# Loop matmuls on 64-row by 32-column tiles with swapped row halves, and table additions by accumulating DMAs

## The chip, the cores and the metric

The kernel runs on one core of one Trainium2 chip. The metric is device time of that core, in microseconds (us). Names of the profile: PE is TensorE, PEld its weight loads, DVE VectorE, ACT ScalarE, POOL GpSimd, SP SyncE.

## What is computed

Two independent layers on a sequence of 2,048 positions and 576 channels, their outputs side by side:

```python
# A: a diagonal state-space layer, as a causal convolution (128 states)
P = exp(dt*A[:, :, None] * l)                  # 576 x 128 x 2048, complex
K = einsum("dn,dnl,dn->dl", C, P, dt*B).real   # a kernel of 2048 taps for each channel
y = causal_conv(u, K) + u * Dskip              # by FFT in the reference
# B: attention, 32 heads of 18, one shared key and value head
q, k, v = x @ wq, x @ wk, x @ wv
p = softmax(q @ k.T * 18**-0.5)
out = concat_heads(p @ v) @ wo
```

## The kernel before, in words

**Attention** is one long loop over 4 chunks of 512 queries, 8 groups of 4 heads, 16 blocks of 128 keys and the 2 pairs of heads in a group: 1,024 exponentials of 128 x 1,024 elements on ACT (L538, L536). Ahead of each stands a *score* `s` on PE (L527: 8 matmuls in fp16 on tiles of 64 rows by 32 columns, 512 columns each), into one of two PSUM slots. After two exponentials stands a *product* `ops` (L836: 8 fp32 matmuls on tiles of the same shape, 512 columns each; an fp32 matmul shows as two records, each with its weight load). The P buffers between are ten.

**Everything else on PE is filler** between scores and products, and before the change it runs on tiles of 128 rows by 32 columns, four matmuls at a time (`matmul4`, L203): the query projection `q` (`qproj`, L418: 10 units of 256 columns for each of 19 blocks, half as many in the narrow fifth ones), the output projection `op` (`outproj`, 3 chunks x 40 units of 288 columns, and `outproj_part`, 24 units for the fourth chunk), and the convolution's three kinds: `kg` (L1260, the taps of a block of channels from two tables), the transforms `lu`, `hu`, `lk`, `hk` of input and taps, and the inverse `iy`. A unit is one visit of a filler to PE, or a part of it. The contraction of 576 channels is four blocks of 128 rows and one of 64, padded with zeros to 128.

**PSUM**: two double banks for scores, one for `ops`, one bank "a" for attention's fillers and one bank "c" for the convolution's. A filler's result is read out by DVE before its bank is filled again.

**The convolution's tables** are made on DVE (`tables`): 12 blocks of 48 channels, each in 2 parts; for each part a low table of 24 x 24 elements in a partition and a high table in two pieces of 24 x 32 and 24 x 24. A complex product costs three multiplications and two additions (L128), so each of the three pieces is five passes. `kgen` multiplies low by high.

**The order** of PE, ACT and DVE is written by a planner at build time (`main`, with the model clock `Clock`). It keeps a model time for PE, DVE and ACT and takes at each step the next score, product or filler unit; the engines then run their lists in order. It adds 0.12 us to the model whenever the row count of the tiles changes (`Clock.tile`, SWITCH). Before the change it puts a filler first where ACT has work enough left, then a score whose slot is free, then a product whenever one is due. The convolution is held to a pace of DVE work for each step (RATE = 1.9). POOL and SP issue the DMAs; POOL's are the stores of projected queries to DRAM (`qd`, L468, L506).

## Time and profile before

| | |
|---|---|
| median of 3 runs | 1172.84 us (1171.32 to 1174.79) |
| profiled execution, own time | 1173.67 us |
| its span, first to last instruction | 1171.9 us |
| granted TensorE clock, mean | 0.991 |
| DMA, mean | 72 GB/s |

The profile gives the busy time of each engine, groups of instructions by line and tile, who waited for whom, and a timeline in which instructions of one kind in a row are merged (start, time from the first start to the last end, engine, line, names, xcount). Ends of matmuls are modelled, so two starts in a row say more of PE than a duration.

### The profile page before, as it was taken

The numbers are of one execution on the slowest core, as the hardware profiler recorded it, in microseconds if no ns is written. First come the engines' busy times: TensorE is split into PE (matmuls) and PEld (weight loads), VectorE is DVE, ScalarE is ACT, GpSimd is POOL, SyncE is SP. The second block draws the span as 40 slices with busy tenths as digits, with TensorE's granted clock in tenths as the row PEclk, the third lists the DMA queues.
The fourth block names the chain that finished last, engine by engine and source line by source line (L and its number), as shares of the span: only waits on it lengthen the run. The fifth ranks groups of instructions, "written<-read, shape, count | busy, mean of one in ns | idle before, by whom it ended". The sixth has DMA issues, their size and how long they took to land.

```text
span 1171.9 us, 53466 instructions
## 1 busy us (share of the span) xinstructions
PE 1107.6 (95%) x24126; PEld 419.0 (36%) x24126; DVE 1015.0 (87%) x1713; ACT 1040.0 (89%) x1052; POOL 141.6 (12%) x257
## 2 busy tenths in 40 slices
PE   6899999999999999999899999999988999999986
PEld 2333333333333333433333333333333333333323
DVE  4868998998998997998899897998789899799583
ACT  3789999998999998999899999888899999999980
POOL 5303310112210100010401100001120000000000
PEclk9999999999999999999999999999999999999998
DMA  7412512113222003131412202113222210302101
GB/s 222 132 49 80 175 29 83 47 44 103 88 69 96 28 32 97 62 112 29 131 47 89 75 25 75 57 40 82 69 68 74 66 36 22 103 30 76 59 21 65
DMA packets 59358, 84.66 MB, mean 72 GB/s; under 512 B 14867, under 2 KB 35335, under 8 KB 58613
## 3 DMA queue, kind: packets, MB, share of 16 engines
q1 hardware_dynamic: 47557, 73.24, 19.5%
q0 software_dynamic: 10848, 7.37, 2.5%
q8 instruction: 190, 3.11, 1.1%
q10 hardware_dynamic: 720, 0.58, 0.2%
q14 instruction: 43, 0.35, 0.1%
HBM read 46.59 MB, written 33.85 MB: 69 GB/s over the span
## 4 chain that ended last, share of the span: by engine, by line
PE 66%; ACT 19%; DVE 7%; issue 4%; DMA 3%; SPq 0%; ACTq 0%; DVEq 0%
PE ops L836 24%; ACT P L538 18%; PE s L527 17%; PE q L418 6%; PE op L203 5%; PE iy L203 3%; PE kg L1260 3%; PE lk L203 2%; PE hk L203 1%; PE lu L203 1%; PE hu L203 1%; DMA xr<-xT 1%; ACT P L536 1%; PE fin L203 1%; DVE t L128 1%
## 5 line engine op out<-in xcount | busy, mean ns | idle before, releaser
L538 ACT ACTIVATE P<-s 128x1024 f32<-128x1024 f32 x992 | 975.8, 1028 | 69.3 <-PE ops L836 17.8
L836 PE MATMUL ops<-P,v_sb 64*32 64x512 f32 x8192 | 539.2, 593 | 1.9 <-DVE u L1050 1.4
L527 PE MATMUL s<-aug,kaug 55*32 55x512 f16 x8192 | 417.6, 383 | 33.1 <-ACT P L538 28.0
L527 PEld LDWEIGHTS <-kaug 55*32 55x32 f16 x8192 | 134.9, 90 | 386.8 <-issue 375.9
L836 PEld LDWEIGHTS ops<-P,v_sb 64*32 64x32 f32 x8192 | 146.9, 106 | 75.8 <-issue 46.0
L468 POOL DMA_DIRECT2D qd<-qh x116 | 66.2, 578 | 412.9 <-DVE qh L136 410.0
L418 PE MATMUL q<-x,wq_sb 128*32 128x256 f32 x1360 | 104.1, 389 | 0.4 <-DVE un L144 0.4
L203 PE MATMUL op<-wo_sb,oT 126*32 126x288 f32 (+1 forms) x1056 | 88.2, 416 | 0.0
L128 DVE TENSOR_TENSOR tab<-tab,tt 128x576 f32<-128x576 f32 (+1 forms) x72 | 59.2, 822 | 2.0
L128 DVE TENSOR_TENSOR tab<-fr,dif 128x576 f32<-128x576 f32 (+1 forms) x72 | 58.7, 815 | 0.0
L128 DVE TENSOR_TENSOR tt<-fr,sum 128x576 f32<-128x576 f32 (+1 forms) x72 | 58.7, 815 | 0.0
L128 DVE TENSOR_TENSOR tab<-sum,fr 128x576 f32<-128x576 f32 (+1 forms) x72 | 58.7, 815 | 0.0
L128 DVE TENSOR_TENSOR tab<-tab 128x576 f32<-128x576 f32 (+1 forms) x72 | 58.6, 814 | 0.0
L418 PEld LDWEIGHTS q<-x,wq_sb 128*32 128x32 f32 x1360 | 29.4, 108 | 71.5 <-issue 64.2
L1171 POOL MEMSET fr<- 128x192 f32 x24 | 9.9, 495 | 371.5 <-DVE tt L128 239.4
L203 PE MATMUL iy<-w,dft_sb 128*32 128x192 f32 x768 | 41.6, 340 | 8.6 <-DVE u L128 8.6
L128 DVE TENSOR_TENSOR acc<-acc,pt 128x1728 f32<-128x1728 f32 (+2 forms) x36 | 48.7, 1354 | 0.7
L128 DVE TENSOR_TENSOR pt<-us,ks 128x1728 f32<-128x1728 f32 (+2 forms) x36 | 48.0, 1351 | 0.3
L536 ACT ACTIVATE P<-s,bias 128x1024 f32<-128x1024 f32 x32 | 32.9, 1124 | 16.6 <-PE s L527 10.6
L132 DVE COPY ksb<-kg 128x192 f32<-128x192 f32 x48 | 17.3, 360 | 33.3 <-PE kg L1260 33.0
L203 PEld LDWEIGHTS op<-wo_sb,oT 126*32 126x32 f32 (+1 forms) x1056 | 22.9, 108 | 60.7 <-issue 50.7
L1260 PEld LDWEIGHTS kg<-tab 128*32 128x32 f32 x2304 | 35.0, 110 | 25.0 <-issue 14.6
(167 smaller groups left out, 1039.5 us busy)
## 6 DMA issues: line engine op xcount, KB each, us to landing
od<-o SPq DMA_DIRECT2D x31, 256.0 KB
aug<-qd SPq DMA_DIRECT2D x124, 55.0 KB
u<-u SPq DMA_DIRECT2D x12, 384.0 KB
kd<-ksb SPq DMA_DIRECT2D x12, 384.0 KB
kt<-kd SPq DMA_DIRECT2D x48, 96.0 KB
outa<-u SPq DMA_DIRECT2D x12, 384.0 KB
pw<-pw SPq DMA_DIRECT2D x8, 528.0 KB
oT<-od SPq DMA_DIRECT2D x16, 252.0 KB
```

Source lines behind the costliest of these rows:

```text
L128: return self.v.tensor_tensor(out, *a, **k)
L132: return self.v.tensor_copy(out, *a, **k)
L203: nc.tensor.matmul(ps[j:e], w[:, j:e], x, start=start, stop=stop, tile_position=(0, j))
L418: nc.tensor.matmul(ps[o, 256 * f:256 * f + 256], w[:, k, i], xt[:, k, x], start=(k == 0), stop=(k == 4), tile_position=(0, 32 * j))
L468: q.dma_start(qd[h:h + n, row + d:row + d + nd, cs], src[i1:i1 + n * nd, :cs.stop - cs.start])
L527: nc.tensor.matmul(ps[e:e + 32, j, :], self.kaug[r, kb * P + e:kb * P + e + 32], t[r, :], start=True, stop=True, tile_position=(64 * j, e))
L536: nc.scalar.activation(pt, ps, AF.Exp, bias=self.bias, scale=SCALE / QQ)
L538: nc.scalar.activation(pt, ps, AF.Exp, scale=SCALE / QQ)
L836: nc.tensor.matmul(o_ps[32 * j:32 * j + 32, b, cs], self.v[r, kb, :], pts[2 * pi + j // 2][r, j % 2, cs], start=(kb == 0), stop=(kb == 15) ...
L1171: nc.gpsimd.memset(t[:, :, 0:NF:8], one)
L1260: nc.tensor.matmul(ps[32 * g:32 * g + 32, d, :], t[:, :32], t[:, 32:], start=(j == 0), stop=(j == 1), tile_position=(0, 32 * g))
```

## The change

**Tiles.** All fillers of the loop run on tiles of 64 rows by 32 columns (`halves`): eight matmuls at once, the upper 64 rows of the contraction for one half of the output columns into one PSUM bank, the lower 64 rows for the other half into the next bank; then, in a second pass, the row halves are swapped, so that each bank gets the rest of its sum. So a unit holds twice as many matmuls over the same number of streamed columns for each. Between the two passes of a result stands a `drain` of PE (`flush`): once for each of 19 `q`, 12 `op`, 12 `op` parts, 24 `kg`, 48 transforms (now `dtu` and `dtk`) and 12 `iy`, 127 in all. The 64 real rows of the last contraction block are now held twice, in both halves of the partitions, so that `q` and the three whole chunks of `op` have 9 units where they had 10 (weights and rows of `op` are laid out anew for that). Only the small `up` and the tail's `fin` stay on 128 rows.

**PSUM.** The banks "a" and "c" become one pair of banks, which one filler at a time holds, from its first unit until DVE has read it.

**Tables.** The two high pieces keep their three multiplications (on halves of 24 x 32 and 24 x 24), but the additions go: two DMAs issued by POOL add on arrival, each 128 x 1,344 elements of fp32, the second of them after the first, since it writes what the first reads. The sign is moved into the factors (`sum`, now in two operations). Four small copies stand where two stood. The planner takes the tables for usable 9 us (LANDS) after the last multiplication of the high pieces; the low piece is made in that time.

**Planner.** P buffers 9 for 10; RATE 2.5 for 1.9; a score whose slot is free comes first (unless DVE is about to run dry), and a product or filler starts only where it ends within 0.2 us of the moment at which the model's ACT, less 0.3 us, has nothing left. Setup loads the double rows by a few more DMAs; `wo` is loaded in the new layout and once more in the old for the last chunk.

The core of the diff:

```diff
-NP = 10
+NP = 9
...
-RATE = 1.9
+RATE = 2.5
...
-DRY = 1.0
-ENTER = 0.7
-EDGE = 0.25
-STAY = 0.4
+DRY = 0.6
+EDGE = 0.3
+URGE = 0.2
+OVER = 0.2
...
+LANDS = 9.0
...
-    def tile(self, rows):
-        if rows != self.tiling:
-            self.tiling, self.t = rows, self.t + SWITCH
...
+def halves(nc, ps, cols, w, x, swap, start, stop):
+    for j in range(0, P, 32):
+        for b in range(2):
+            r, i = slice(64 * b, 64 * b + 64), b ^ swap
+            nc.tensor.matmul(ps[j:j + 32, i, cols], w(r, i, j), x(r, i, j), start=start, stop=stop, tile_position=(64 * b, j))
...
-        self.ps_f = {b: pool(f"ps_f{b}", 1, space=PSUM) for b in "ac"}
+        self.ps_f = pool("ps_f", 1, space=PSUM)
...
+    def pair(self, n, name):
+        self.k.pe(0.0, self.k.fill)
+        t = self.ps_f.tile([P, 2, CT], F32, tag="f", name=name)
+        return t[:, :, :n]
+    def flush(self):
+        self.nc.tensor.drain()
+        self.k.pe(0.12)
...
+        for swap, k in [(0, k) for k in range(5)] + [(1, k) for k in range(4)]:
+            def wi(r, i, j):
+                return w[r, k, j:j + 32] if m < 4 else w[r, k, j % 64:j % 64 + 32]
+            def xi(r, i, j):
+                x0 = 256 * i if m < 4 else 256 * (j // 64) + 128 * i
+                return xt[r, k, x0:x0 + n]
+            if (swap, k) == (1, 0):
+                self.flush()
+            halves(nc, ps, slice(0, n), wi, xi, swap, (swap, k) == (0, 0), (swap, k) == (1, 3))
+            K.pe(0.43 * n / 256)
+            self.q_left -= n / 256
+            self.units += n / 256
...
+            ps = self.pair(288, f"op{c}_{t}")
+            for swap, k in [(0, k) for k in range(5)] + [(1, k) for k in range(4)]:
+                if (swap, k) == (1, 0):
+                    self.flush()
+                halves(nc, ps, slice(0, 288), lambda r, i, j: o[r, k, t * P + j:t * P + j + 32],
+                       lambda r, i, j: w[r, k, 288 * i:288 * i + 288], swap, (swap, k) == (0, 0), (swap, k) == (1, 3))
...
+            last = (K.a if si < n_s else 1e9) - EDGE
+            st = choose()
+            if free <= K.t and not (st is not None and st is not side and K.v < K.t + DRY and K.t + 0.45 <= last + URGE):
+                score()
+                continue
+            if wanted(st) and K.t + 0.45 <= last + (URGE if st is not side and K.v < K.t + DRY else OVER):
                 conv.count(st)
-            elif free <= K.t:
-                score()
-            elif due() <= K.t:
+            elif due() <= K.t and K.t + 0.86 / SPLIT <= last + OVER:
                 product()
+            elif st is not None and K.t + 0.45 <= last + OVER:
+                conv.count(st)
             else:
...
+        add = lambda out, x: nc.gpsimd.dma_start(flat(out), flat(x), accum_op=ALU.add)
+        halves = ((0, 4), (4, 7))
+        for j0, j1 in halves:
+            tt(hi[:, 1, 1 + j0:1 + j1], L(r, j1 - j0), H(df, 1, j0, j1), op=ALU.mult)
             yield "v", 0.0, False
-            tt(re, L(sm), H(r), op=ALU.mult)
+            tt(hi[:, 0, 1 + j0:1 + j1], L(sm, j1 - j0), H(r, 17, j0, j1), op=ALU.mult)
+            if j0:
+                add(hi[:, 1, 1:], hi[:, 0, 1:])
             yield "v", 0.0, False
-            tt(t, L(f), H(sm), op=ALU.mult)
+        for j0, j1 in halves:
+            tt(t[:, j0:j1], L(f, j1 - j0), H(sm, 17, j0, j1), op=ALU.mult)
+            if j0:
+                add(hi[:, 0, 1:], t)
             yield "v", 0.0, False
-            tt(im, im, re, op=ALU.add)
-            yield "v", 0.0, False
-            tt(re, re, t, op=ALU.subtract)
-            if (lo, j0) != (8, 4):
-                yield "v", 0.0, False
+        self.tab_ready = K.v + LANDS
+        for j, x in enumerate((r, f)):
+            V.tensor_copy(lo[:, j, :, 0:8], x[:, :, 0:8])
+            V.tensor_copy(hi[:, j, 0], x[:, :, 8:16])
...
+        ps = self.at.pair(n * 64, f"kg{k}_{s}")
+        for swap in range(2):
+            for d in range(n):
+                at = lambda i, j: j // 32 * TB + i * n + d
+                for x in range(2):
+                    if (swap, d, x) == (1, 0, 0):
+                        self.at.flush()
+                    halves(nc, ps, slice(64 * d, 64 * d + 64), lambda r, i, j: lo[r, x, at(i, j), :], lambda r, i, j: hi[r, x, :, at(i, j), :],
+                           swap, (swap, d, x) == (0, 0, 0), (swap, d, x) == (1, n - 1, 1))
+            K.pe(0.665)
+            if swap == 0:
+                yield "p", 0.0, True
...
+            ps = self.at.pair(2 * NE, f"dt{nm}{j}")
+            for swap, h in ((0, 0), (0, 1), (1, 0), (1, 1)):
+                if (swap, h) == (1, 0):
+                    self.at.flush()
+                halves(nc, ps, slice(h * NE, h * NE + NE), lambda r, i, e: self.dft[r, (4 * j + 2 * h + i) * P + e:(4 * j + 2 * h + i) * P + e + 32],
+                       lambda r, i, e: src(r, 2 * h + i), swap, (swap, h) == (0, 0), (swap, h) == (1, 1))
+                K.pe(0.33)
+                if (swap, h) != (1, 1):
+                    yield "p", 0.0, True
+            self.evacuate()
+            V.tensor_copy(x, ps[:, :, NE:])
+            V.tensor_tensor(ac[:, 2 * j:2 * j + 2, :], ps[:, :, 0:NE], x, op=ALU.add)
+            V.tensor_tensor(bd[:, 0:4:3, :] if j == 0 else bd[:, 1:3, :], ps[:, :, 0:NE], x, op=ALU.subtract)
+            self.evacuated()```

On PE, at the taps of a block (`kg`, third block, between the scores `s` of two key blocks; the second number after the names is columns). Before:

```order
L527 MATMUL s_7_5_2712<-aug_115,kaug 32x512
L1260 MATMUL kg_0_0_2723<-tab_0_2425 32x64 [waits DVE_49]
L1260 MATMUL kg_0_0_2723<-tab_0_2425 32x64 x23
...
L836 MATMUL ops_3_2588<-P_6_4_2666,v_sb 32x512 x4
L836 MATMUL ops_3_2588<-P_7_4_2682,v_sb 32x512 x4
...
L1260 MATMUL kg_0_1_2782<-tab_0_2425 32x64 [waits DVE_49]
L1260 MATMUL kg_0_1_2782<-tab_0_2425 32x64 x23
```

And after the change, at the same block:

```order
L550 MATMUL s_7_5_3084<-aug_112,kaug 32x512
L205 MATMUL kg_0_3097<-tab_0_2737 32x64 [waits DMASW0_49,DVE_49]
L205 MATMUL kg_0_3097<-tab_0_2737 32x64 x7
L205 MATMUL kg_0_3097<-tab_0_2737 32x64 [waits DMASW7_49]
L205 MATMUL kg_0_3097<-tab_0_2737 32x64 x39
...
L205 MATMUL kg_0_3097<-tab_0_2737 32x64 x48
```

Two results of 24 matmuls have become one of 96, in two halves of 48; its first matmul waits for the two adding DMAs (DMASW) where it waited for DVE alone, and the second half stands one score later with no product between.

On DVE, the passes of one table (`tab`; `tt` and `th` are the third products). Before, the two high pieces:

```order
L128 TENSOR_TENSOR tab_0_4122<-fr_3761,dif_4007 128x24x32
L128 TENSOR_TENSOR tab_0_4122<-sum_4006,fr_3761 128x24x32
L128 TENSOR_TENSOR tt_0_8_0_4253<-fr_3761,sum_4006 128x768 [waits DVE_49]
L128 TENSOR_TENSOR tab_0_4122<-tab_0_4122 128x24x32 [waits DVE_49]
L128 TENSOR_TENSOR tab_0_4122<-tab_0_4122,tt_0_8_0_4253 128x24x32 [waits DVE_49]
L128 TENSOR_TENSOR tab_0_4122<-fr_3761,dif_4007 128x24x24
L128 TENSOR_TENSOR tab_0_4122<-sum_4006,fr_3761 128x24x24
L128 TENSOR_TENSOR tt_0_8_4_4335<-fr_3761,sum_4006 128x576 [waits DVE_49]
L128 TENSOR_TENSOR tab_0_4122<-tab_0_4122 128x24x24 [waits DVE_49]
L128 TENSOR_TENSOR tab_0_4122<-tab_0_4122,tt_0_8_4_4335 128x24x24 [waits DVE_49]
```

After, the high pieces and the start of the low one, in the table that the `kg` above reads:

```order
L121 TENSOR_TENSOR tab_0_2737<-fr_2392,dif_2650 128x768 [waits DMAHW6_49,DMAHW5_49,DVE_49]
L121 TENSOR_TENSOR tab_0_2737<-sum_2649,fr_2392 128x768
L121 TENSOR_TENSOR tab_0_2737<-fr_2392,dif_2650 128x576
L121 TENSOR_TENSOR tab_0_2737<-sum_2649,fr_2392 128x576
L121 TENSOR_TENSOR th_0_2738<-fr_2392,sum_2649 128x768
L417 MEMSET wo_sb 1x5
L121 TENSOR_TENSOR th_0_2738<-fr_2392,sum_2649 128x576
L125 COPY tab_0_2737<-fr_2392 128x24x8
L125 COPY tab_0_2737<-fr_2392 128x192
```

The four additions are gone, the six multiplications stand in a row, and the low piece, which was first, comes last.

On POOL, after the change, the adding DMAs of that table and what is queued behind them:

```order
L529 DMA qd_299<-sh_4_2619 4x2x256 [waits DMASW6_49,DVE_49]
L1274 DMA tab_0_2737<-tab_0_2737 128x1344 [waits DMASW7_49,DMAHW5_49,DVE_49,DMAHW6_49,PE_49,Activation_49]
L1274 DMA tab_0_2737<-th_0_2738 128x1344 [waits DMASW7_49,DMASW0_49,DVE_49]
L491 DMA qd_2913<-qh_0_2907 7x18x512 [waits DMASW1_49,DVE_49]
L491 DMA qd_2913<-qh_0_2907 2x512 [waits DMASW2_49]
```

Before, POOL's list held only the stores of queries and small memsets there. The second addition waits for the first to land (DMASW0), and the stores of the next projected queries stand behind it.

373 lines of the change are left out of this document (183 added, 190 removed).

## The prediction

> **What bounds the kernel now.** First the page's totals, and the busy time in the loop (40 to 1137 us) and in the tail:
>
> ```profile
> PE 1107.6 (95%) x24126; PEld 419.0 (36%) x24126; DVE 1015.0 (87%) x1713; ACT 1040.0 (89%) x1052; POOL 141.6 (12%) x257
> 40.00:1137.00 1097.00, 1058.32 (x23456) 398.20 (x23440) 979.32 (x1620) 1019.83 (x1030) 121.07 (x216) 1.00 0.22 68
> 1137.00:1172.00 35.00, 20.89 (x312) 10.52 (x308) 13.18 (x25) 0.66 (x2) 0.00 (x0) 0.84 0.16 56
> ```
>
> In the loop PE is busy 1058 of 1097 us (96.5%, at full clock), DVE 979 (89%), ACT 1020 (93%). ACT's share hides slack, as its timeline shows:
>
> ```profile
> 1123.69 13.09 ACT L538 ACTIVATE P<-s 128x1024 f32<-128x1024 f32 x14
> 175.71 24.89 ACT L538 ACTIVATE P<-s 128x1024 f32<-128x1024 f32 x23 [0.16 <-PE s L527]
> L538 ACT ACTIVATE P<-s 128x1024 f32<-128x1024 f32 x992 | 975.8, 1028 | 69.3 <-PE ops L836 17.8 <-PE s L527 15.4 <-ACT P L538 1.0
> ```
>
> One exponential lasts 1.03 us, but neighbours overlap: in the first run they start (13.09 - 1.03)/13 = 0.93 us apart, in the second (24.89 - 1.03)/22 = 1.08. Where the 1.08 comes from shows PE's timeline:
>
> ```profile
> 1126.76 0.41 PE L527 MATMUL s<-aug,kaug 55*32 55x512 f16 x8
> 1127.10 0.69 PE L203 MATMUL op<-wo_sb,oT 126*32 126x288 f32 x8
> 1127.72 0.41 PE L527 MATMUL s<-aug,kaug 55*32 55x512 f16 x8
> 1127.95 1.04 PE L836 MATMUL ops<-P,v_sb 64*32 64x512 f32 x16
> 1128.81 0.95 PE L527 MATMUL s<-aug,kaug 55*32 55x512 f16 x16
> ...
> 1156.52 1.64 PE L203 MATMUL fin_o<-wo_sb,oT 126*32 126x288 f32 x24
> 1157.97 1.16 PE L203 MATMUL fin<-w,o_last 128*32 128x288 f32 x16
> ```
>
> From start to start: a score 0.23, a product 0.86, together 1.09 from score to score, which is the slow run's pace. A score followed by a filler takes 0.34, and the filler 0.62 to the next score, while the same unit among its like (`fin_o`, three units of 288 columns) takes 1.45/3 = 0.48. So a visit of one `op` to PE costs 0.11 + 0.14 = 0.25 us beyond its matmuls. The `kg` agrees:
>
> ```profile
> 1089.79 0.40 PE L527 MATMUL s<-aug,kaug 55*32 55x512 f16 x8
> 1090.12 0.88 PE L1260 MATMUL kg<-tab 128*32 128x64 f32 x48
> 1090.92 0.41 PE L527 MATMUL s<-aug,kaug 55*32 55x512 f16 x8
> ```
>
> A product streams 512 columns in 0.86 us, 1.68 ns a column, so six groups of 64 columns should take 0.65; they take 0.80, and the score ahead of them 0.33: again 0.25. The waits are small beside that:
>
> ```profile
> PE s L527 <- ACT P L538: 28.0, 71, 1.3
> ACT P L538 <- PE ops L836: 17.8, 19, 1.7
> ACT P L538 <- PE s L527: 15.4, 38, 1.8
> ```
>
> So PE paces the loop, and a part of what it does is the change of tile shape.
>
> **The change, part by part, against the profiled execution (1173.67 us, 0.83 above the median of the runs shown).**
>
> *Changes of shape.* In PE's order before the change, 445 of the 1,023 gaps between two scores hold a filler on 128 rows. At 0.25 us: 111 us of PE time removed (20 `up` keep theirs, within the rounding). No work hides it, since PE is the engine that ACT waits for.
>
> *Units.* 15 `q` of 0.43 us (256 columns), 4 narrow halves of 0.21 and 12 `op` of 0.48 go: 13 us. The other units stream the same columns; I take them at the rate of the product, whose tiles have the new shape.
>
> *The 127 drains.* The trace has none in the loop. Lower bound: one side of a change of shape, 0.11. Upper bound, from these rows:
>
> ```profile
> L203 PE MATMUL iy<-w,dft_sb 128*32 128x192 f32 x768 | 41.6, 340 | 8.6 <-DVE u L128 8.6
> L1260 PEld LDWEIGHTS kg<-tab 128*32 128x32 f32 x2304 | 35.0, 110 | 25.0 <-issue 14.6
> ```
>
> an `iy` record lasts 0.34 us of which 0.16 are streaming, so 0.18 to empty the array, and 0.11 for a weight load that can no longer be fetched early: 0.29. I take 0.15, near the change of shape, since that too empties the array: 19 us (14 to 37).
>
> PE's need in the loop: 1058 - 111 - 13 + 19 = **953 us** (948 to 971).
>
> *DVE.* By form, the additions that go:
>
> ```profile
> L128 DVE TENSOR_TENSOR tab<-tab,tt 128x576 f32<-128x576 f32 x48 | 36.3, 756 | 1.3
> L128 DVE TENSOR_TENSOR tab<-tab 128x576 f32<-128x576 f32 x48 | 35.9, 747 | 0.0
> L128 DVE TENSOR_TENSOR tab<-tab,tt 128x768 f32<-128x768 f32 x24 | 22.9, 955 | 0.6
> L128 DVE TENSOR_TENSOR tab<-tab 128x768 f32<-128x768 f32 x24 | 22.8, 949 | 0.0
> L132 DVE COPY tab<-fr 128x384 f32<-128x384 f32 x48 | 14.8, 349 | 0.0
> L132 DVE COPY fr<-pw 128x192 f32<-128x192 f32 x36 | 9.3, 357 | 2.5 <-DMA pw<-pw 2.5
> ```
>
> Half of the two 576 groups (the low piece keeps its own) and both 768 groups: 18.2 + 18.0 + 22.9 + 22.8 = 82 us. Against it, four copies of 192 elements for two of 384, 24 x (4 x 0.36 - 2 x 0.35) = 18, and a second pass for `sum`, about 2. Need: 979 - 82 + 20 = **917 us**.
>
> *ACT* does the same work: 1,024 x 0.93 = 952, and the three bursts of sines, each three activations and two table loads:
>
> ```profile
> L1128 ACT ACTIVATE stage<-stage,hp_sb 128x2112 f32<-128x2112 f32 (+1 forms) x3 | 5.7, 1910 | 0.0
> L1128 ACT ACT_TABLE_LOAD x3 | 3.8, 1283 | 0.1
> ```
>
> 3 x 5.7 + 2 x 3.8 = 25. Some exponentials lie ahead of 40 us: the need in the loop is about **970 us**.
>
> *The new length of the loop.* No engine is now the bound by itself. ACT's 970 is a floor; PE at its present 96.5% would give 988. I do not expect that, because both need almost the whole time, there are only two score slots, and each filler's result waits for DVE. DVE's share is what the planner has so far lived with: 917/0.89 = 1030. There PE is busy 92.5% and ACT 94%. I take 1030: **-67 us**, with 988 (-109) and 1044 (drains at 0.29 and PE at 93%; -53) as ends.
>
> *The adding DMAs.* Landing is bounded by:
>
> ```profile
> q1 hardware_dynamic: 47557, 73.24, 19.5%
> qd<-qh POOLq DMA_DIRECT2D x24, 108.0 KB, 3.0
> qd<-qh POOLq DMA_DIRECT2D x16, 27.0 KB, 2.6
> ```
>
> One addition moves 128 x 1,344 x 4 bytes = 672 KB. From POOL's stores, 0.4 us for 81 KB more, it is 2.6 + 3.2 = 5.8 us; from the rate of q1 (73.24 MB in 19.5% of 16 engines' 1172 us, 320 KB/us) 2.6 + 2.1 = 4.7; if reading the target doubles the first price's bytes, 9.0. I take 5.3, between the two plain prices. The second waits for the first and is ready 1.7 us after it (0.95 + 0.75 for the third products), so the tables are whole 2 x 5.3 - 1.7 = 8.9 us after the last high product, against 9 in the plan. Behind the `kg` that comes early stand PE's next scores and so ACT; behind the second addition on POOL stand the stores of queries, which are fetched tens of us later. I count 5 us for the few late ones (0 to 15): **+5**. DMA: Bandwidth & Descriptors of the Trainium skill (Anatomy of one DMA) prices a POOL-issued DMA at 2.0 us and its bytes at 436 GB/s, which would be an estimate of 3.6 us each and 5.5 for the chain; by that the 5 us would be 0. No run here shows it yet.
>
> *Tail.* The last result of the convolution stands between the last scaled rows and the final projection:
>
> ```profile
> 1142.02 0.77 SPq L575 DMA_DIRECT2D db<-rden  x1
> 1146.23 0.69 DVE L128 TENSOR_TENSOR oT<-oT,db 126x512 f32<-126x512 f32 x1 [6.50 <-DMA db<-rden]
> 1147.44 2.79 PE L203 MATMUL iy<-w,dft_sb 128*32 128x192 f32 x32 [7.89 <-DVE u L128]
> 1150.00 3.51 PE L203 MATMUL fin<-wo_sb,oT 126*32 126x288 f32 x48
> ```
>
> With RATE 2.5 the convolution ends inside the loop and `fin` can start at about 1147: **-3**. The wait for `db` stays. The setup's extra DMAs and the second load of `wo` fall beside other work: 0 (at most 1 without that cover).
>
> Sum: 1173.7 - 67 + 5 - 3 = 1108.7; less 0.8 for the median: **1108 us**. Own range 1063 (-109 - 3) to 1135 (-53 + 15 - 0).
>
> **Rivals.**
>
> *The tables land late* (ends slower). PE takes its list in order: a `kg` whose second addition has not landed stops scores too, and ACT runs dry after the two slots. The forecast's gain is 67 us over 24 tables, so it is gone where PE loses 2.8 us at each, that is with tables 11.8 us after the last high product, or 6.8 us for an addition. At 9.0 the chain is 16.3, the loss 24 x 7.3 = 175 and the time 1280. For it: 6.8 lies between my bounds, and POOL's DMAs share engines with q1. Against it: the DVE order has, from the last high product to the copy of `kg`, at these durations 12 us of work or more in 19 of 24 places, so most `kg` stand later than the plan's 9. Chance 0.12; time about 1207 with additions of 7.5 us (24 x 4.3 = 103 lost).
>
> *One pair of banks.* Each of 127 results holds the only pair while DVE reads it: three passes like `scu<-hu` at 0.55, and the pass that DVE is in. Where nothing but scores is ready then, PE idles about 0.3 to 0.5 us. For it: in the new order 157 gaps between scores hold nothing, against 101. Price 127 x 0.35 = 44: 1152. It decides from about 0.5 us a result, where the forecast's spare PE time of 7% is used up. Chance 0.09.
>
> *Issue.* Fillers have twice the matmuls. If a record took as long as in `kg` now (0.65 us for 48, 14 ns), 192 records would take 2.7 us for 1.3, 24 x 1.4 = 33 us: 1141. Against it:
>
> ```profile
> 1127.72 0.11 PEld L527 LDWEIGHTS <-kaug 55*32 55x32 f16 x8 [0.47 <-issue]
> L527 PEld LDWEIGHTS <-kaug 55*32 55x32 f16 x8192 | 134.9, 90 | 386.8 <-issue 375.9
> ```
>
> eight loads of 90 ns lie within 0.11 us, so they start 3 ns apart on tiles of this shape. Chance 0.06. TensorEngine Tiling (Array Packing) of the Trainium skill (Instruction Overhead) speaks against the change here: about 60 cycles a matmul, and no tiling where a dimension is already small; `kg` streams only 64 columns. The 14 ns a record that this trace shows for `kg` are under the 25 ns that 60 cycles would be (an estimate, at the 2.4 GHz of TensorE: Matmul & The Clock Gate of the Trainium skill, its table of specifications), so by this trace the cost is not paid in series across tiles.
>
> *No change.* The planner, now short of a bank and of a P buffer, gives the time back: 1170 to 1176. Chance 0.03.
>
> **How the numbers follow.** The forecast holds 0.70. Range 1064 to 1155: the forecast's own and the rivals of 1141 and 1152, leaving out the late tables and a little on the low side. Faster by over 0.3% (3.5 us, about what a measurement of this kernel can tell): 0.70 + 0.09 + 0.06 = 0.85; same 0.03; slower 0.12.
>
> **What would show it.** In the new profile: score to filler 0.23 instead of 0.34, units at 0.43, 0.48 and 0.32; PE's idle before the first matmul of a second pass, 0.11 to 0.29 a drain; landing of the additions near 5.3 us and few waits of PE for them; DVE near 955 in all; runs of exponentials at 0.93 with a filler between. I am wrong if PE waits for the adding DMAs by tens of us, if ACT's runs stay near 1.0 although PE idles, or if PE's units are longer than the product's rate gives.

## The result, and the profile after

The changed kernel takes 1295.66 us in the median of 4 runs (1290.77 to 1300.99) against 1173.82 of the kernel before beside it: 1.1035 times as long, 95% interval 1.0979 to 1.1091. The forecast was 1108, with a range of 1064 to 1155, so it is missed on the wrong side, by 188 us. Of the runs below, one execution of the kernel before with nine buffers took 5,880 us and is left out of its median; nothing recorded says why.

The totals of the page after, and the windows of the loop (here 40 to 1265 us) with busy time of PE, weight loads, DVE, ACT and POOL, then granted clock, DMA share and GB/s:

```profile
PE 1094.6 (85%) x31070; PEld 585.5 (45%) x31070; DVE 952.4 (74%) x1654; ACT 1026.5 (80%) x1052; POOL 183.7 (14%) x304
40.00:1265.00 1225.00, 1053.83 (x30496) 569.29 (x30480) 918.01 (x1564) 1009.36 (x1033) 163.69 (x264) 0.97 0.35 89
```

DVE has the work that I forecast (952 in all against 955), and ACT does as much as before. But the loop is 1225 us long where it was 1097, and no engine is full in it: PE 86%, ACT 82%, DVE 75%. So the 128 us are waits. What the engines waited for (total, times, longest):

```profile
ACT P L561 <- PE s L550: 177.0, 164, 6.8
PE s L550 <- ACT P L561: 45.7, 105, 1.5
PE s L550 <- issue: 29.4, 16, 4.1
PE kg L205 <- issue: 25.2, 21, 2.0
PE ops L879 <- issue: 11.5, 10, 2.2
PE kg L205 <- DMA tab<-th: 10.0, 3, 5.8
PE q L205 <- issue: 5.9, 8, 2.2
```

ACT waits 177 us for scores, where it waited 15. PE waits for the adding DMAs (`tab<-th`) only 10 us. The new kind of row is "issue": PE stands still, for up to 4 us, in the middle of its list and waits for nothing that the profile shows. Before the change no PE row of this kind is among its waits; now they come to 86 us over nine kinds of tile, of which the four largest are shown. Two such places in PE's and ACT's timeline, the first in a score, the second in a `kg`:

```profile
827.95 0.38 PE L550 MATMUL s<-aug,kaug 55*32 55x512 f16 x1
830.82 0.41 PE L550 MATMUL s<-aug,kaug 55*32 55x512 f16 x7 [2.50 <-issue]
831.38 1.02 ACT L561 ACTIVATE P<-s 128x1024 f32<-128x1024 f32 x1 [2.71 <-PE s L550]
...
1217.64 1.10 PE L205 MATMUL kg<-tab 64*32 64x64 f32 x88
1220.42 0.26 PE L205 MATMUL kg<-tab 64*32 64x64 f32 x4 [1.68 <-issue]
```

One matmul of a score starts, the other seven 2.9 us later, and ACT idles 2.7 us. In `kg`, 88 records start within 0.88 us (10 ns apart; before, 48 took 0.80 up to the next score) and then the list stops for 1.7 us. What is under way in the pause of the score, from 828.4 to 830.8 us, by DMA queue (packets, MB, share):

```profile
q8 instruction: 1, 0.02, 2.5%
```

That queue brings the instructions, 16 KB at a time: 245 packets in the whole execution after, 190 before. In the 3.9 us ahead of that pause it brought none; the packet comes while PE stands still, and PE goes on 1.3 us after its end. So the reading that I took into the experiments was: PE runs out of instructions. The whole trace bears it out. It puts 54 gaps of PE of over 0.3 us (81 us together) down to "issue", and each of them ends 1.2 to 1.6 us after the end of such a packet. For the pause in `kg` above, the packet lies between 1217.7 and 1219.0 us:

```profile
q8 instruction: 1, 0.02, 5.3%
```

The packets' 4.01 MB over PE's 62,140 records and weight loads are 65 bytes each (before the change 3.11 MB over 48,252, 65 bytes too), so one packet holds about 127 records with their weight loads. At 10 ns a record `kg` uses that up in 1.3 us, and at these pauses 2.2 us or more pass from the start of a packet until PE goes on. By this estimate a dense stretch uses instructions faster than a packet brings them. The Trainium skill, Runtime: NRT & Kernel Launch (Instruction fetch mechanics), says that the sequencer fetches blocks of 16 KiB by a DMA queue of its own while it works, and that the fetch is hidden; this trace agrees on the blocks and not on the hiding.

What came as forecast: the visits. From score to filler 0.21 to 0.22 us, two units of `q` in 0.86, two of `op` in 0.97:

```profile
347.83 0.41 PE L550 MATMUL s<-aug,kaug 55*32 55x512 f16 x8
348.04 1.06 PE L205 MATMUL q<-x,wq_sb 64*32 64x256 f32 x32
348.90 0.41 PE L550 MATMUL s<-aug,kaug 55*32 55x512 f16 x8
...
1009.06 1.17 PE L205 MATMUL op<-wo_sb,oT 64*32 64x288 f32 x32
1010.03 0.41 PE L550 MATMUL s<-aug,kaug 55*32 55x512 f16 x8
```

### The profile page after: what moved, and what is told of

It is laid out like the page before. It is cut to its first block, busy times and chain, and to the rows that moved or that the text cites. A ratio compares the mean times of both kernels' runs of the same rounds, so it can differ in the third digit from the quotient of the medians.

```text
span 1288.9 us, 67604 instructions
## 1 busy us (share of the span) xinstructions
PE 1094.6 (85%) x31070; PEld 585.5 (45%) x31070; DVE 952.4 (74%) x1654; ACT 1026.5 (80%) x1052; POOL 183.7 (14%) x304
## 5 line engine op out<-in xcount | busy, mean ns | idle before, releaser
L561 ACT ACTIVATE P<-s 128x1024 f32<-128x1024 f32 x992 | 962.2, 1033 | 211.1 <-PE s L550 177.0
L879 PE MATMUL ops<-P,v_sb 64*32 64x512 f32 x8192 | 576.6, 604 | 13.8 <-issue 11.5
L550 PE MATMUL s<-aug,kaug 55*32 55x512 f16 x8192 | 481.1, 386 | 86.1 <-ACT P L561 45.7
L550 PEld LDWEIGHTS <-kaug 55*32 55x32 f16 x8192 | 188.7, 91 | 349.8 <-issue 320.6
L879 PEld LDWEIGHTS ops<-P,v_sb 64*32 64x32 f32 x8192 | 180.8, 108 | 108.2 <-issue 72.9
L205 PE MATMUL q<-x,wq_sb 64*32 64x256 f32 (+1 forms) x2736 | 92.8, 358 | 7.8 <-issue 5.9
L205 PE MATMUL kg<-tab 64*32 64x64 f32 x4608 | 66.5, 236 | 38.1 <-issue 25.2
L205 PE MATMUL op<-wo_sb,oT 64*32 64x288 f32 x2112 | 89.8, 404 | 6.1 <-issue 3.9
L1274 POOL DMA_DIRECT2D tab<-tab x24 | 23.0, 957 | 491.7 <-DVE tab L121 228.6
L491 POOL DMA_DIRECT2D qd<-qh x116 | 67.5, 662 | 161.9 <-DVE qh L129 155.3
L205 PEld LDWEIGHTS kg<-tab 64*32 64x32 f32 x4608 | 57.5, 111 | 57.3 <-issue 50.8
L125 DVE COPY ksb<-kg 128x192 f32<-128x192 f32 x48 | 15.1, 360 | 89.1 <-PE kg L205 79.1
L205 PEld LDWEIGHTS q<-x,wq_sb 64*32 64x32 f32 x2736 | 52.5, 107 | 32.5 <-issue 18.1
L125 DVE COPY scu<-dtu 128x384 f32<-128x384 f32 x24 | 13.4, 557 | 63.7 <-PE dtu L205 63.5
L121 DVE TENSOR_TENSOR tab<-fr,dif 128x576 f32<-128x576 f32 (+1 forms) x72 | 58.8, 817 | 0.4
L121 DVE TENSOR_TENSOR tab<-sum,fr 128x576 f32<-128x576 f32 (+1 forms) x72 | 58.8, 816 | 0.0
L205 PE MATMUL dtu<-u,dft_sb 64*32 64x192 f32 x1536 | 51.1, 334 | 8.9 <-issue 3.7
L205 PEld LDWEIGHTS op<-wo_sb,oT 64*32 64x32 f32 (+1 forms) x2112 | 42.6, 106 | 34.1 <-issue 21.7
L205 PE MATMUL dtk<-kt,dft_sb 64*32 64x192 f32 x1536 | 50.0, 326 | 6.2 <-DMA kt<-kd 1.5
L121 DVE TENSOR_TENSOR acc<-acc,pt 128x1728 f32<-128x1728 f32 (+2 forms) x36 | 48.7, 1353 | 0.6
L121 DVE TENSOR_TENSOR pt<-us,ks 128x1728 f32<-128x1728 f32 (+2 forms) x36 | 47.7, 1351 | 0.3
L205 PE MATMUL iy<-w,dft_sb 64*32 64x192 f32 x1536 | 42.2, 324 | 6.7 <-issue 3.0
```

The source lines that it names most:

```text
L121: return self.v.tensor_tensor(out, *a, **k)
L125: return self.v.tensor_copy(out, *a, **k)
L205: nc.tensor.matmul(ps[j:j + 32, i, cols], w(r, i, j), x(r, i, j), start=start, stop=stop, tile_position=(64 * b, j))
L491: q.dma_start(qd[h:h + n, row + d:row + d + nd, cs], src[i1:i1 + n * nd, :cs.stop - cs.start])
L550: nc.tensor.matmul(ps[e:e + 32, j, :], self.kaug[r, kb * P + e:kb * P + e + 32], t[r, :], start=True, stop=True, tile_position=(64 * j, e))
L561: nc.scalar.activation(pt, ps, AF.Exp, scale=SCALE / QQ)
```

## The experiments

Each time is a median of several runs, beside the kernel before on the same chip (1171.5 to 1174.5); the ratio is to that kernel, with its 95% interval.

### First four: drains, adding DMAs, neither

Without the adding DMAs:

```diff
-        add = lambda out, x: nc.gpsimd.dma_start(flat(out), flat(x), accum_op=ALU.add)
+        add = lambda out, x: None
```

> The changed kernel with the 24 adding DMAs left out (the tables lack the added half, so those sums are incomplete; the order of every engine's instructions stays as it was). Theory A (each drain stops PE and also uses up the lead of its instruction supply, so that PE runs out of instructions in 48 pauses of 89 us): the pauses stay, only the waits for the late tables go, 10 us: about 1285. Rival B (the instruction fetches are slowed by the adding DMAs, and the pauses are theirs): the 89 us of pauses and the 10 us of waits go, about 1196. Rival C (the pauses come from the number and density of PE instructions alone, whatever drains and DMAs do): 1285 too. Rival D (the tables land late, as in my prediction's rival): a gain of more than 40 us, below 1255.

Measured: 1215.8 us, 1.0339 (1.0316 to 1.0361), 80 us less than the changed kernel. PE's "issue" waits fall from 86 to 53 us, and those in `kg` stay:

```profile
PE kg L205 <- issue: 22.7, 18, 2.7
PE s L550 <- issue: 14.4, 9, 3.9
```

Theory A is wrong about the adding DMAs: they cost 80 us and not 10. B is right in part only, since 53 us of pauses stay; the gain is one that D allows.

Without the drains:

```diff
-            r, i = slice(64 * b, 64 * b + 64), b ^ swap
+            r, i = slice(64 * b, 64 * b + 64), b
...
-        self.nc.tensor.drain()
```

> The changed kernel without the 127 drains; so that none is needed, the second pass multiplies the same row halves into the same banks again (half of each filler sum is left out, the count and shapes of the matmuls and the order are the same, and the flag that would choose the general version is set to 1). Theory A: 39 us of drain idle and most of the 89 us of pauses go, 1165 to 1185. Rival B: only the 39 us, about 1257. Rival C: 39 us, about 1257, with the pauses still 48 or so.

Measured: 1261.8 us, 1.0748 (1.0691 to 1.0806): 34 us less. The "issue" waits stay, at 84 us, so what goes is the drains' own idle time, 34/127 = 0.27 us each. Theory A falls: drains don't cause the pauses.

Both edits at once:

> Both of the above: no adding DMA and no drain, in the changed kernel's order. Theory A: as without the drains and 10 us less, 1155 to 1175. Rival B: 39 + 89 + 10 us less, about 1158, but then most of that has to show without the adding DMAs alone. Rival C: 49 us less, about 1247.

Measured: 1181.3 us, 1.008 (1.0048 to 1.0112), 114 us less: the two costs add up, 80 and 34.

The kernel before with 127 drains, for example in the middle of a half of `kg`:

```diff
             for d in range(TB // 2):
+                if (q, d) == (0, TB // 4):
+                    nc.tensor.drain()
```

> The kernel before with 127 drains added, one in each filler result where the changed kernel has its second pass begin (19 in q, 24 in op, 24 in kg, 48 in the transforms, 12 in iy), and nothing else. Theory A: 127 x 0.30 us = 38 us of idle, and pauses of the instruction supply as in the changed kernel, so 1211 plus 20 to 90: 1230 to 1300. Rivals B and C: 38 us at most and no pauses, 1195 to 1211, since PE has 61 us in which it waits for ACT anyway.

Measured: 1201.5 us, 1.0237 (1.022 to 1.0255): 27 us, with next to no pauses (1.6 us of "issue"). One drain can be read off PE's timeline of this kernel, where the first half of each `kg` has one and the second has none:

```profile
1116.32 1.20 PE L1268 MATMUL kg<-tab 128*32 128x64 f32 x48
1117.45 0.41 PE L529 MATMUL s<-aug,kaug 55*32 55x512 f16 x8
...
1118.87 0.88 PE L1268 MATMUL kg<-tab 128*32 128x64 f32 x48
1119.67 0.41 PE L529 MATMUL s<-aug,kaug 55*32 55x512 f16 x8
```

From the half's start to the next score 1.13 us with the drain and 0.80 without: 0.33 us a drain, and 27/127 = 0.22 us of it, as a mean, reach the end.

### Adding, copying, and kg by itself

The same DMAs, copying:

```diff
-        add = lambda out, x: nc.gpsimd.dma_start(flat(out), flat(x), accum_op=ALU.add)
+        add = lambda out, x: nc.gpsimd.dma_start(flat(out), flat(x))
```

> The changed kernel in which the 48 DMAs of 672 KB copy instead of adding (the tables then hold one of the two terms in place of the sum; queue, bytes, order and waits are the same). Where the 80 us went that leaving them out gave back: theory P, the bytes in flight hold up the fetches of PE's instructions and the tables land late whether they are added or copied: 1275 to 1300, as the changed kernel. Rival Q, the adding on arrival itself is what is slow (it reads, adds and writes): 30 to 80 us come back, 1215 to 1265.

Measured: 1231.0 us, 1.0516 (1.0482 to 1.0549). As many bytes in the same order cost 15 us (21 by the ratios) where adding costs 80, so it is the adding on arrival that is dear. PE's "issue" waits are as without the DMAs, 51 us. An adding DMA also lands later. Issue to landing in us (last column), the changed kernel first, then this one:

```profile
tab<-tab POOLq DMA_DIRECT2D x24, 672.0 KB, 6.0
tab<-th POOLq DMA_DIRECT2D x24, 672.0 KB, 6.0
```

```profile
tab<-tab POOLq DMA_DIRECT2D x24, 672.0 KB, 3.5
tab<-th POOLq DMA_DIRECT2D x24, 672.0 KB, 3.8
```

The estimate of 3.6 us that the prediction took from the Trainium skill, DMA: Bandwidth & Descriptors (Anatomy of one DMA), is that of the copy. Collectives: The Full Stack of the Trainium skill (The bandwidth ceiling: the fold count and why AG ≠ RS ≠ AR) says of a collective's adding step that it has half the rate of a copying one because the addition needs two source reads. 6.0 us against 3.5 agrees in direction; no run here shows the reads.

`kg` alone back on 128 rows:

```diff
-        for swap in range(2):
+        for q in range(2):
...
-                    halves(nc, ps, slice(64 * d, 64 * d + 64), lambda r, i, j: lo[r, x, at(i, j), :], lambda r, i, j: hi[r, x, :, at(i, j), :],
-                           swap, (swap, d, x) == (0, 0, 0), (swap, d, x) == (1, n - 1, 1))
+                    for g in range(4):
+                        i = g * TB + q * n + d
+                        nc.tensor.matmul(ps[32 * g:32 * g + 32, q, 64 * d:64 * d + 64], lo[:, x, i, :], hi[:, x, :, i, :],
+                                         start=(x == 0), stop=(x == 1), tile_position=(0, 32 * g))
...
-            if swap == 0:
+            if q == 0:
```

> The changed kernel with kg alone back on 128-row tiles: 2,304 matmuls in place of 4,608 and 24 drains fewer, all else as changed. Theory K (kg asks for its instructions faster than they are brought in: 27 pauses of 40 us begin in it or right behind it, and its records come 13 to 14 ns apart in place of the 13.9 us of two halves at 0.665): the pauses near kg go, 40 us, its own time shrinks by 20, the drains by 7, and 24 to 48 visits with changes of tiling come back for 0.2 us each, 8: about 1235. Rival C (the number of instructions over the whole loop empties the supply, wherever they are): the pauses move to other places, 1270 to 1290.

Measured: 1232.5 us, 1.0508 (1.047 to 1.0547), 63 us less than the changed kernel, as theory K has it; C falls. Waits of PE in `kg` and scores:

```profile
PE kg L1320 <- DMA tab<-th: 20.7, 8, 8.2
PE s L550 <- issue: 8.1, 9, 2.4
PE kg L1320 <- issue: 4.8, 4, 2.8
```

"issue" in `kg` falls from 25.2 to 4.8 us and in scores from 29.4 to 8.1, and the late tables come out behind it (20.7 where it was 10.0). Over all tiles "issue" falls from 86 to 36 us. The records themselves were not dearer: in the median, half a result on 64 rows takes 0.95 us up to the next score and the score ahead of it 0.22, together 1.17; here they take 0.81 and 0.34, together 1.15. So the 63 us are pauses (50 us less) and 24 drains (about 7 us), not the records' own time. This is the place that the rule of TensorEngine Tiling (Array Packing) of the Trainium skill (Instruction Overhead) speaks of, named in the prediction: no tiling where a dimension is already small. It was right on `kg`, though the price per record is 10 ns here and not its 60 cycles.

`kg` on 128 rows, and the additions by DVE:

```diff
-LANDS = 9.0
+LANDS = 0.3
...
-        add = lambda out, x: nc.gpsimd.dma_start(flat(out), flat(x), accum_op=ALU.add)
+        add = lambda out, x: tt(out, out, x, op=ALU.add)
```

> The changed kernel with kg on 128-row tiles and the two additions done by DVE in place of the DMAs; the drains of the other results stay. Theory K and P together: 1216 (without adding DMAs) less 60 for kg, and 48 additions of about 1.4 us on DVE, 67 us that lie mostly under PE: 1150 to 1180, the first of these versions that could be below the kernel before. Rival: DVE, back at about 1020 us of work, ends later than PE and the time stays at 1190 to 1215.

Measured: 1212.0 us, 1.0337 (1.031 to 1.0364). The rival was right: DVE's additions are not hidden. They are 48 of 1.56 us each, 75 us, in two groups of this run (by form; busy, mean ns of one):

```profile
L121 DVE TENSOR_TENSOR tab<-tab,th 128x1344 f32<-128x1344 f32 x24 | 37.4, 1558 | 0.8
L121 DVE TENSOR_TENSOR tab<-tab 128x1344 f32<-128x1344 f32 x24 | 37.4, 1558 | 0.8
```

### The change taken apart

`kg` on 128 rows and no additions at all, with the drains and then without:

> The changed kernel with kg on 128-row tiles and the two additions of the high tables left out altogether (those sums lack a term); drains stay in the other results. If the cost of the adding DMAs (80 us) and that of kg's dense instructions (63 us) are two separate things, they add up: 1296 - 80 - 63 = 1153, and the pauses of the supply are all but gone. If they are one thing counted twice (late instructions matter only where kg is dense), it stays at 1195 to 1215.

Measured: 1158.4 us, 0.9867 (0.9844 to 0.989). The costs are separate and add up, and 13 us of "issue" are left. This is the case that the prediction's loop was worked out for, but for `kg`. Its exponentials end at 1140 us; the loop, 40 to 1140, and two waits of the whole run:

```profile
40.00:1140.00 1100.00, 1014.79 (x28328) 529.67 (x28319) 921.82 (x1578) 1007.25 (x1033) 119.72 (x216) 0.99 0.23 69
ACT P L561 <- PE s L550: 52.4, 110, 4.8
PE s L550 <- ACT P L561: 46.9, 111, 0.9
```

With 75 us of additions gone the loop is as long as before the change (1097), with DVE busy in 84% of it, PE and ACT in 92%. ACT waits longer for scores than before (52 us for 15) and PE longer for ACT (47 for 28).

> The same, and the drains too taken out, with the second pass on the same row halves again (half of each filler sum is left out): what is left is the 64-row tiling and the new order alone. My prediction's mechanism (the gaps with a filler become 0.25 us shorter) should then show: 1153 - 30 = about 1120 to 1130, some 45 to 55 us below the kernel before. Rival: the saved switches only turn into waits for ACT and for DVE, and the time is that of the kernel before, 1160 to 1180.

Measured: 1127.3 us, 0.962 (0.9573 to 0.9668). As expected, and at first sight my mechanism, worth 47 us. That PE's shorter visits alone do not bring it is shown by the last run of all, which has DVE's additions again and differs from this one by them and by the LANDS that goes with them:

> The changed kernel's 64-row tiles and order by themselves: kg on 128-row tiles, DVE's additions in place of the DMAs, no drains (second pass on the same row halves again, so half of each filler sum is left out). All of DVE's work is there again, as in the kernel before. If shorter gaps are worth what I forecast, PE's need falls by 110 us: 1110 to 1140. If PE's saved switches are worth the 47 us by which 1127 lies below the kernel before: the additions' 54 us are hidden here and it stays at 1127 to 1145. If DVE paces the loop as much as PE does, so that the 47 us came from the additions that were left out: 1127 + 54 = 1181, no better than the kernel before, 1170 to 1190.

Measured: 1192.7 us, 1.0172 (1.0145 to 1.0199). So the 64-row tiles and their order, with kg on 128 rows, with all of DVE's work and without drains, are 20 us slower than the kernel before; a buffer less costs 9 us in the old order, as a control below shows. What the additions do there: first the windows 40 to 1100 and ACT's last exponentials without them, then with them, and two waits of PE there:

```profile
40.00:1100.00 1060.00, 986.88 (x28236) 524.74 (x28244) 919.74 (x1577) 995.16 (x1028) 119.82 (x216) 1.00 0.24 72
1094.51 11.66 ACT L560 ACTIVATE P<-s 128x1024 f32<-128x1024 f32 x12 [0.27 <-PE s L549]
```

```profile
40.00:1100.00 1060.00, 966.96 (x27084) 507.78 (x27076) 945.83 (x1552) 969.35 (x1001) 119.88 (x216) 0.98 0.23 69
1079.81 54.35 ACT L560 ACTIVATE P<-s 128x1024 f32<-128x1024 f32 x57
PE iy L205 <- DVE w L121: 22.4, 1, 22.4
PE kg L1319 <- DVE tab L121: 15.1, 10, 2.3
```

Without the additions the exponentials end at 1106.2 and the span at 1124.1; with them at 1134.2 and 1192.1. The loop is 28 us longer and the tail 40 (58 in place of 18), since the convolution is not done when the loop ends: its last `iy` waits 22 us for DVE alone. In the loop `kg` waits 15 us for DVE's tables. PE's clock is lower there too, 0.98 against 1.00 in these windows, which is some 20 us of its time at most. DVE is busy 945.83/1060 = 89% there, the share that it had in the kernel before. Before, the loop ended at 1137: with all of DVE's work the new tiling brings 3 us there, or 10 against the kernel before with nine buffers, whose exponentials end at 1144.

### The adding DMAs by themselves

The kernel before with the changed kernel's 9 buffers, as a control, and with 48 adding DMAs into a tile that nobody reads. (A version with ten buffers and two such tiles gave no time: it left 31.3 KB a partition of SBUF for buffers that need 40. Its expectation was that of the next run: 1174 to 1205 by theory P, 1225 to 1255 by rival R.)

> The kernel before with 9 in place of 10 buffers for the exponentials, as the changed kernel has, and nothing else: the control of the next run, and of that part of the change by itself. 1172 to 1185; if the tenth buffer mattered much, more.

Measured: 1183.8 us, 1.0074 (1.0051 to 1.0097): the tenth buffer was worth 9 us.

> The same with 48 DMAs of 672 KB that add into one spare tile, issued on the same queue at the same places of the table work as in the changed kernel; nothing reads the spare tile and no table waits for it. Theory P, they hold up PE's instruction fetches, and PE before takes its instructions at a lower rate, with a longer supply in hand: 0 to 30 us over the control. Rival R, they slow down everything alike: 50 to 80 us over the control.

Measured: 1334.4 us, 1.1386 (1.1344 to 1.1429), a worse result than any theory had, and no answer: nothing tied the DMAs to their tables, and all 48 stood at the head of POOL's queue, with the stores of queries and the memsets for DVE behind them. POOL's and DVE's waits show it:

```profile
POOL spare L1250 <- DMA spare<-dft_sb: 213.1, 41, 8.9
DVE qh L136 <- DMA qd<-qh: 65.4, 2, 54.9
```

So each pair was tied to its table by a one-element write of DVE:

```diff
...
+                if j0 == 0:
+                    V.memset(self.spare[0:1, 0:1], 0.0)
+                nc.gpsimd.dma_start(self.spare, self.dft[:, d0:d0 + 1344], accum_op=ALU.add)
```

> The kernel before with 9 buffers and 48 DMAs of 672 KB that add into a spare tile nobody reads, as in the last run, but two per table, each pair held back by a one-element write of DVE, so that it starts when its table is made (there all 48 stood at the head of the queue of GpSimd and ran one behind another up to 370 us). Control: 1184.6. Theory P (they hold up PE's instruction fetches; before, PE draws instructions more slowly and has a supply in hand): 1184 to 1205. Rival R (they slow down everything alike): 50 to 80 us over the control, 1235 to 1265.

Measured: 1202.7 us, 1.0256 (1.0239 to 1.0273): 19 us over the control, within theory P's range. PE's "issue" waits, of which the control has none, begin, but they are only 4 of the 19 us:

```profile
PE s L527 <- issue: 1.7, 2, 1.2
PE kg L1268 <- issue: 1.2, 2, 0.6
```

In the changed order, with kg on 128 rows, the same was done with the real data, again beside a control (8 buffers, to make room):

> The run with kg on 128-row tiles and without additions (1158), with 8 in place of 9 buffers for the exponentials: control of the next run only. 1158 to 1185.

Measured: 1172.5 us, 0.9986 (0.9971 to 1.0).

> As the control, with the 48 adding DMAs of the changed kernel at their places, but adding the same data into a spare tile that nobody reads: nothing waits for them, and the tables hold one term only. If the DMAs' cost (1232 with them, 1158 without) is that they hold up PE's instructions: 40 to 75 us over the control. If it is the tables that are waited for, or the numbers in them: 0 to 25 us over the control.

Measured: 1232.2 us, 1.0473 (1.0424 to 1.0521): 60 us over the control, though no table waits for a DMA. PE's waits, the control first:

```profile
PE dtk L205 <- issue: 3.6, 13, 1.7
PE q L205 <- issue: 2.7, 4, 2.2
PE kg L1320 <- issue: 0.6, 1, 0.6
```

```profile
PE kg L1327 <- issue: 13.7, 10, 2.9
PE ops L879 <- issue: 6.4, 8, 1.9
```

Over all tiles "issue" rises from 14 to 45 us, half of the 60. The pauses stand where the DMAs are: 23 of the 28 over 0.3 us end behind an instruction packet that starts while an adding DMA is under way, though only 52 of all 227 packets start then. In the run with plain copies it is 3 of 36. The packets themselves take no longer (1.0 us in the median in both runs), so it is their start that is late; the profile does not show why.

So of the 74 us that adding DMAs cost in this order (1232.5 against 1158.4), some 60 are the DMAs as such (with 8 buffers), and half of these are pauses of PE's supply. What the other half is, the runs do not show.

The late tables, by the planner's allowance:

```diff
-LANDS = 9.0
+LANDS = 14.0
```

> The changed kernel with the planner's allowance for the adding DMAs raised from 9 to 14 us, so that kg is placed later. The two additions take 6.0 us each one behind the other, 10.5 to 11 us behind the last product. If part of their 80 us is that the table is waited for (26 us of waits on semaphores more than without them), 15 to 26 us come back: 1270 to 1281. If their cost is the held-up fetches alone: 1290 to 1300.

Measured: 1300.8 us, 1.1077 (1.1049 to 1.1106): no gain. `kg` now never waits for `tab<-th`, but the convolution, placed later, ends behind the loop:

```profile
PE iy L205 <- DVE w L121: 22.4, 1, 22.4
```

The loop ends at 1236 us in place of 1265, and the tail behind it is 66 us in place of 24. So this run can't tell by itself what the late tables cost: what was won there was paid at the end. The nearest figure for them is what is left of the 74 beside the 60.

The additions by GpSimd's own engine:

```diff
-        add = lambda out, x: nc.gpsimd.dma_start(flat(out), flat(x), accum_op=ALU.add)
+        add = lambda out, x: nc.gpsimd.tensor_tensor(out, out, x, op=ALU.add)
```

> The changed kernel with kg on 128-row tiles and the two additions done by GpSimd (48 additions of 128x1344 numbers) in place of the DMAs. Nothing then passes through the DMA engines and DVE has no more work: if GpSimd is as good as free (it is busy 14%), this is the run without additions, 1158, plus a few late tables: 1158 to 1175, level with the kernel before or below it. Rival: GpSimd's additions take several us each, so that tables come late and the waits of the qd DMAs behind them on its queue grow, or they slow DVE down beside them: 1185 to 1230.

Measured: 1216.6 us, 1.0364 (1.0347 to 1.0382): the rival. GpSimd takes 4.4 and 3.3 us an addition, and DVE beside it slows down; the third row (by form) is one of DVE's own products, 750 ns in the run without additions:

```profile
L1274 POOL TENSOR_TENSOR tab<-tab 128x1344 f32<-128x1344 f32 x24 | 105.6, 4402 | 422.2 <-DVE tab L121 345.5 <-PE s L550 48.8 <-DVE dn L129 19.7
L1274 POOL TENSOR_TENSOR tab<-tab,th 128x1344 f32<-128x1344 f32 x24 | 78.2, 3258 | 13.4 <-DVE th L121 11.8 <-DVE un L137 0.8
L121 DVE TENSOR_TENSOR tab<-sum,fr 128x576 f32<-128x576 f32 x48 | 51.9, 1081 | 0.0
```

And one control of a side idea, the run with DVE's additions with each sum put elsewhere:

```diff
-        add = lambda out, x: tt(out, out, x, op=ALU.add)
+        add = lambda out, x: tt(t, out, x, op=ALU.add)
```

> As the run with DVE's additions and kg on 128-row tiles (1212), but DVE writes each sum into the scratch tile in place of the table: the work and the order are the same, while the tables hold one term only, as in the run without additions (1158, whose granted clock was 0.992 where that of the runs with complete tables was 0.964 to 0.977). If the 54 us between those two are DVE's 55 us of work: about 1212. If the numbers in the tables matter (a lower clock with the complete sums), the clock comes back to 0.99 and the time to 1180 to 1195.

Measured: 1214.3 us, 1.0331 (1.0304 to 1.0357), as with the sums in place (1212.0). The numbers in the tables don't matter. The 55 us of the expectation are not the additions: that group of the page mixes one of the two with an addition of the low piece, which every version makes. Taken by form they are 75 us, of which 54 show in the time.

## Why the prediction was wrong, point by point

The runs that differ by one step each take the 122 us apart:

| step | us after it | change |
|---|---|---|
| kernel before | 1174 | |
| 64-row tiles, new order, 9 buffers, kg on 128 rows, DVE's additions kept, no drains | 1193 | +19 |
| additions left out (and LANDS 9) | 1127 | -65 |
| drains | 1158 | +31 |
| adding DMAs | 1232 | +74 |
| kg on 64 rows | 1296 | +63 |

Against the forecast of 1108, the miss of 188 us has three parts. Without the DMAs and with `kg` on 128 rows the kernel takes 1158, where the sum without its +5 gives 1103: 55 us. The DMAs cost 74 where the sum had 5: 69 us. `kg` on 64 rows costs 63 where the sum had nothing.

- *Changes of shape, 111 us of PE time.* The visits did become 0.25 us shorter. That this shortens the loop failed: "PE paces the loop" was read from PE's 96.5% of busy time. With PE relieved, DVE's work kept and no drains at all, the loop ends 3 us earlier and the tail is longer.
- *The new length of the loop, 1030 us by DVE's share of 89%.* This step failed. With DVE's work as low as forecast (955 forecast, 952 measured) and the drains in, the loop is 1100 long at a share of 84%; without drains it is 1066. The prediction named the reason, that PE and ACT both need most of the time and meet over two score slots, but it sized it by DVE's share so far; measured, ACT waits 52 us for scores and PE 47 for ACT. Still, DVE is where the gain lies that did come: leaving out its 75 us of additions is worth 65 us once PE is relieved. The kernel before without additions was not run, so what DVE's relief is worth alone is not shown.
- *Tail, -3.* Without additions and drains it is 18 us in place of 35, since the convolution is done in time; where DVE keeps its additions it is 58.
- *Drains, 19 us (14 to 37).* 31 in this order (103 of them, without those in kg), 34 for all 127. The upper bound of 0.29 was the right one; one visit shows 0.33.
- *The adding DMAs, +5.* The term that was furthest off. The landing (6.0 us against 5.3) was only a little off, and PE's waits for the tables are 10 us, so the rival of late tables, as I had it, is not what happened. What I did not have at all is that they are in the way of others: 74 us, some 60 of them with no table waiting, and half of these in pauses of PE's instructions.
- *Issue, 33 us at a chance of 0.06.* The rival named the right place, with the wrong mechanism, and its chance was too small. I priced the records at 14 ns; they came 10 ns apart and cost no more time than before. The 63 us are the pauses behind them and the drains. My evidence against it, eight loads 3 ns apart, was a burst of 8, and `kg` is one of 192.
- *ACT at 0.93.* 54.35 us for 57 exponentials are (54.35 - 1.03)/56 = 0.95 us, with fillers between. In such a stretch this held.
- *What would have shown me wrong:* tens of us of PE waiting for DMAs did not come. The sign was ACT waiting for scores, 177 us, and PE's own waits "issue", which I had not listed.

Shown by the runs: each of the table's prices, in its order, that drains don't cause the pauses, that the dense `kg` and the adding DMAs do, that adding costs more than copying. Shown by the trace: that the pauses are an empty instruction supply, since all 54 end behind a packet of the instruction queue, at nearly the same distance. Argued: why DVE's additions cost what they do. The waits for DVE and its share of 89% speak for DVE as the pace, but LANDS changes with them, and so does the clock.

The granted clock is 0.985 to 0.992 in the profiled runs of the new order without additions or with copies, and 0.964 to 0.979 in those with additions by DMA, DVE or GpSimd. In the changed kernel's trace it is either 1.0 or 0.5. Each of its 14 stretches at 0.5 ahead of the last microseconds (3.4 or 6.8 us long) has PE idle for 1.7 to 3.9 us of the 5 us before it. In the run with DVE's additions and no drains one such stretch of 23.9 us lies in the tail, where `iy` waits for DVE. So the lower clock follows PE's waits, as far as these traces tell. At 0.976 against 0.991, as in the changed kernel and the one before, it is at most 1.5% of PE's 1050 us, 16 us.

Open: how an adding DMA delays an instruction packet, and the half of its 60 us that is not in pauses. Dropping the drains while keeping the swap was not tried. No version here with the complete computation is below the kernel before.

## What to carry to other kernels

A busy share of 96% does not make an engine the bound: take its work away in the plan and ask which engine's list ends last then. Here relieving PE alone brought nothing, and relieving DVE as well 65 us. And price how two engines wait for each other before both are planned at over 90%. Halving the rows of a tile doubles the instructions; where a matmul streams only 64 columns, that cost 63 us here, since the instructions did not come fast enough. Work given to DMAs is not free because nobody waits for it: 48 adding DMAs held up the instruction packets too.

## What the runs showed of the hardware

- PE's list can stop for up to 4 us for want of instructions: 86 us in the changed kernel, where a stretch of `kg` draws 88 records with their weight loads in 0.88 us. A packet of 16 KB holds about 127 such records, and PE goes on 1.2 to 1.6 us after its end.
- A drain of PE costs 0.27 to 0.33 us of its time, and 0.22 of the kernel's in the old order.
- A DMA of 672 KB within the core that adds on arrival lands in 6.0 us, one that copies in 3.5 to 3.8. In the changed order 48 of them cost 74 to 80 us and 15; 48 adding ones cost 19 in the old order.
- GpSimd's addition of 128 x 1,344 fp32 numbers takes 3.3 to 4.4 us against DVE's 1.56, and beside it one of DVE's products of 128 x 576 slows down from 750 to 1081 ns.
